# Another opening for a state-space and gated-unit kernel: single tiles, smaller first weight loads, tanh gates

## The chip, the cores and the metric

The kernel runs on one core of a Trainium2 chip. A core has five engines, each with its own instruction queue: TensorE (PE in the profile; PEld is its loading of weights), VectorE (DVE), ScalarE (ACT), GpSimd (POOL) and SyncE (SP, which here only issues transfers). They run side by side and wait for each other through semaphores. The on-chip memory SBUF feeds all of them; matrix products land in PSUM, which has eight banks. The metric is the device time of one execution in microseconds (us); lower is better.

## The reference

For 2048 tokens of width 448 the reference adds to the input the product of two branches, both computed from the layer-normed input:

```python
xn = (x - mean(x)) / sqrt(var(x) + 1e-5)

dt      = exp(log_dt)                          # branch s, 448 complex states
Lam_bar = exp(dt * Lam)
Bu      = xn @ (((Lam_bar - 1) / Lam)[:, None] * Bmat).T
h[t]    = Lam_bar * h[t - 1] + Bu[t]
s       = 2 * real(h @ Cmat.T) + xn * Dskip

g = silu((sigmoid(xn @ w_gate) * (xn @ w_up)) @ w_down)      # 1792 hidden columns

out = x + s * g
```

Inputs and output are bf16.

## The kernel before

**Tiles.** The 2048 tokens are four chunks of 512 (`TC`), a chunk is four tiles of 128 tokens, and half a chunk is `HC` = 256. The width 448 is three blocks of 128 rows and one of 64. For each chunk the kernel needs `xnT`, the normed input with its width on the partitions. Chunk 0's is made on PE (`ln_turn`, L268, identity products into the PSUM tile `tp_x`, then a copy to SBUF by VectorE in `ln_out`, L276); those of chunks 1 to 3 are made by transposing DMAs of SP (L265). The last 64 rows of `xnT` stand twice, in the upper and lower half of the partitions, so that products with 64 rows can run side by side in the two halves of PE. The hidden columns are 14 blocks of 128 (`ft`), each with a gate sum and an up sum in a PSUM bank of its own.

**Order.** The order on each engine is the order in which the code is written (`keep_order`, L52): every engine takes its instructions strictly one after the other, so an instruction that waits holds all that stand behind it on its engine.

**The opening** (L933 to L1016) prepares chunk 0 by hand. SP loads x in pairs of tiles (L133, L137), then the first 512 columns of the weights `wg`, `wu` and their last 64 rows `wt` (`load_w`), then the matrices `b_re` and `b_im`, then columns 512 to 1024, then x of chunk 1. ACT's queue loads three rows of parameters. While they come, PE multiplies the identity by itself (`warm`, L192). Means and variances of tiles 0 and 1 come from VectorE (`ln_stats`, L208 and L209), those of 2 and 3 from ACT's sums (L218 to L225); the root is a power on GpSimd (`ln_pow`, L238), one for two tiles. `ln_norm` (L256) writes the normed tile, `norm0` turns it.

In the same time cosines and sines of the state's angles are made for four blocks of states (`pt`), 256 steps each: a count of whole turns by ACT (`emit_whole`, L408) for blocks 0, 1 and 3, the fraction by VectorE (`emit_frac`, L427), for block 2 both on GpSimd (L414 to L419); the magnitude (L435), then sine and cosine on ACT (L440, L443). `emit_steps` (L323) does the same for two single angles, with the chain of small GpSimd operations that ends in `nf` (L330), VectorE's `anf` (L331) and two short sines. VectorE negates the sines (`emit_neg`, L452), GpSimd mirrors the 256 steps into the other half of the tables (`emit_mirror`, L455 to L458).

PE meanwhile sums the first four blocks of gates and ups in halves of 256 tokens (L705, L712). VectorE casts the up sums out of PSUM (`up_copy`, L1000), ACT takes the sigmoid of the gate sums (L717, after a load of its table, 1.28 us), VectorE multiplies (L722).

**The stream.** From L1078 on, `duo` runs two units side by side on the two halves of PE. A unit is one gate-and-up block (number 4 to 13 in chunk 0) or one block of the state's input product (`bu`, written as -1 to -4). A unit needs free banks: unit 4's are those that the first blocks' casts and gates free. The planner spreads VectorE's pieces (scans, rotations) among them; `at(chunk, unit, cost, fn)` hangs other work behind a unit. After unit 6 come the norms of chunk 1 with SP's four transposes, the load of C (`load_c`, L164) and that of `wd` (L1030), which the down products (`emit_downs`, L516 d_ps) at the head of chunk 1's line need whole.

**SP's list.** After the first loads SP issues: two transposes of `b_re` and `b_im` block 0 into `bT` (L291), the weights' columns 1024 to 1792, six more transposes, x of chunk 2, the four transposes of `xnT`, C, `wd`. The last 64 columns of `b_im` are first doubled by two copies (`emit_b_twice`, L282 and L283).

Of the kernel before, what the change touches and what calls it, by code (L numbers as in the profile page):

```python
# [63 lines left out]
def kernel(  # L64
# [35 lines left out]
    xnT = [w.tile([P, KT + 1, TC], BF16, name=f"xnT{c}") for c in range(3)]  # L100
# [32 lines left out]
    sync.dma_start(out=x_t[0][:, 0:2, :], in_=x_src[:, 0:2, :])  # L133
# [4 lines left out]
    load_w(sync, 0, 512)  # L138
# [11 lines left out]
    load_w(sync, 512, 1024)  # L150
    load_x(1)
    sync.dma_start(out=skip[:], in_=A_Dskip.partition_broadcast(P))
# [18 lines left out]
    pool.memset(xn[0][:, :, D:DP], 0.0)  # L171
# [71 lines left out]

    def ln_minus(c):
        t = slice(c * TPC, (c + 1) * TPC)
        dve.tensor_single_scalar(out=nmr[:, t, :], in_=mv[:, t, 0:1], scalar=-1.0, op=ALU.mult)
# [5 lines left out]
    def ln_norm(c, j):  # L252
        t = c * TPC + j
        xb = xn[c % 3]
        if c < 2:
            dve.tensor_scalar(out=xb[:, j, 0:D], in0=x_t[c][:, j, :], scalar1=mv[:, t, 0:1],  # L256
                              scalar2=rsd[:, t, :], op0=ALU.subtract, op1=ALU.mult)
        else:
            act.activation(xb[:, j, 0:D], x_t[c][:, j, :], ACT.Identity, bias=nmr[:, t, :],
                           scale=rsd[:, t, :])  # L260

    def ln_turn(c, j):
        xb, cols = xn[c % 3], slice(j * P, (j + 1) * P)
        if c > 0:
            sync.dma_start_transpose(out=xnT[c][:, 0:KT, cols], in_=xb[:, j, :])  # L265
            return
        for i, f0 in enumerate((0, P, 2 * P, 3 * P, D - P)):
            pe.transpose(tps[j][:, i, :], xb[:, j, f0:f0 + P], ident[:, :])  # L268
# [6 lines left out]
    def ln_out(j, tp, copy):  # L275
        copy(out=xnT[0][:, :, j * P:(j + 1) * P], in_=tp[:])  # L276
# [3 lines left out]
    def emit_b_twice():  # L280
        t = raw["b_im"]
        pool.tensor_copy(out=t[:, 0:3, D:DP], in_=t[:, 0:3, 384:D])  # L282
        pool.tensor_copy(out=t[0:64, 3, D:DP], in_=t[0:64, 3, 384:D])  # L283
# [20 lines left out]

    def emit_vecs():
        tp = ps.tile([P, KT, 4], BF16, name="tp_v", tag="bank", bufs=8)
        turn_twice(tp, rows, 3)
        vec = w.tile([P, KT, 3], FP32, name="vec")
        dve.tensor_copy(out=vec[:], in_=tp[:, :, 0:3])
        dt_b = w.tile([P, KT], BF16, name="dt_b")  # L310
        act.activation(dt_b[:], vec[:, :, 0], ACT.Exp)
        K.update(dt=dt_b, lim=vec[:, :, 1], lre=vec[:, :, 2])
# [10 lines left out]
    def emit_steps():  # L323
# [9 lines left out]
        sn, cs = col("sn", 2 * KT), col("cs", 2 * KT)  # L333
# [78 lines left out]
    def turns_2():  # L412
        K["turns"] = sp.tile([P, HC], FP32, name="turns", tag="tcs")
        pool.tensor_scalar(out=K["turns"][:], in0=iota_f[:], scalar1=K["turn"][:, 2:3], scalar2=None, op0=ALU.mult)  # L414

    def frac_2():
        f = sp.tile([P, HC], FP32, name="frac2", tag="tcs")
        pool.tensor_scalar(out=f[:], in0=K["turns"][:], scalar1=MAGIC, scalar2=-MAGIC, op0=ALU.add, op1=ALU.add)  # L418
        pool.tensor_tensor(out=f[:], in0=K["turns"][:], in1=f[:], op=ALU.subtract)  # L419
        K[2] = f  # L420

    def emit_frac(pt, both=True):
        if pt == 2:
            f = K[pt]
        else:
            f = sp.tile([P, HC], FP32, name="frac", tag="wv")
            dve.scalar_tensor_tensor(out=f[:], in0=iota_f[:], scalar=K["turn"][:, pt:pt + 1], in1=K[pt][:],  # L427
                                     op0=ALU.mult, op1=ALU.subtract)
        K[pt] = f
        if both:  # L430
            emit_abs(pt)
# [99 lines left out]
    def last_rows(c, h):  # L531

        return KT if c == 0 and h else 3

# [8 lines left out]
    def bu_unit(c, pt):  # L543
# [4 lines left out]
        def ops(h, cc, n):  # L548
            lo, hi = bu_cols(pt, cc)
            return [(sums[cc], (bT[HALF[h], kt, lo:hi], xnT[c][HALF[h], kt if kt < 3 else last_rows(c, h), :], 0, TC))  # L550
                    for kt in range(n)]
# [150 lines left out]
    def gu_halves(c, ft, gt, ut, first, n0=0, n1=TC):  # L702
        f0, f1 = ft * P, (ft + 1) * P
        for t, p0 in ((gt, 0), (ut, 64)):
            pe.matmul(t[:, n0:n1], lhsT=wt[p0:p0 + 64, f0:f1],  # L705
                      rhs=xnT[c][p0:p0 + 64, KT if c == 0 and p0 else 3, n0:n1], start=first, stop=not first)

    def gu_wholes(c, ft, gt, ut, first, n0=0, n1=TC):
        f0, f1 = ft * P, (ft + 1) * P
        for t, wm in ((gt, wg), (ut, wu)):  # L710
            for kt in range(3):
# [3 lines left out]
    def gu_out(c, ft, gt, ub):  # L715
        sig = fp.tile([P, TC], BF16, name="sig")
        act.activation(sig[:], gt[:], ACT.Sigmoid)  # L717
        emit_mul()

        def mul():  # L720
            h = fp.tile([P, TC], BF16, name="hF", bufs=18)
            dve.tensor_tensor(out=h[:], in0=sig[:], in1=ub[:], op=ALU.mult)  # L722
            hF[c, ft] = h
# [4 lines left out]
    def gu_unit(c, ft):  # L728
# [6 lines left out]
        def ops(h, i, tail):  # L735
            x = xnT[c]
            o = [(sums[i], ((wg, wu)[i][HALF[h], kt, f], x[HALF[h], kt, :], 0, TC)) for kt in range(3)]
            return o + [(sums[i], (wt[HALF[h], f], x[HALF[h], last_rows(c, h), :], 0, TC))] * tail
# [194 lines left out]
    act.activation(dummy[:], hpi[:], ACT.Exp)  # L933
    ln_sum(2)
    ln_sum(3)
    warm(26)
    ln_stats(0)
    ln_stats(1)
    ln_root(0, 2)
    emit_vecs()  # L940
    ln_mean(2, 2)
    warm(18)
    ln_square(2)
    ln_square(3)
    emit_angles()
    tps = []

    def norm0(j):
        tps.append(ps.tile([P, KT + 1, P], BF16, name="tp_x", tag="bank", bufs=8) if j < 2 else tps[j - 2])
        ln_norm(0, j)  # L950
        ln_turn(0, j)

    norm0(0)
    norm0(1)
    warm(11)
    for pt in (0, 1, 3):
        emit_whole(pt)
    turns_2()
    act.activation(K["r"][:], K["arg"][:], ACT.Exp)
    ln_out(0, tps[0], dve.tensor_copy)  # L960
    ln_root(2, 2, True)
    ln_out(1, tps[1], dve.tensor_copy)
    frac_2()
    emit_frac(0)
    emit_sin(0)
    emit_cos(0)
# [4 lines left out]
    emit_frac(1, False)  # L971
    norm0(2)
    norm0(3)
    emit_abs(1)
    emit_sin(1)
    emit_cos(1)
    ln_out(2, tps[2], dve.tensor_copy)
    ln_out(3, tps[3], dve.tensor_copy)
    gus.append((bank("g_ps"), bank("u_ps")))
    for ft in range(3):  # L980
        gu_halves(0, ft, *gus[ft], False, 0, HC)
    gu_wholes(0, 3, *gus[3], True, 0, HC)
# [5 lines left out]
    for pt in range(2, KT):  # L988
        emit_frac(pt)
        emit_sin(pt)  # L990
        emit_cos(pt)
    emit_steps()
    emit_b_twice()
    for pt in range(KT):
        emit_neg(pt)
        emit_mirror(pt)
    ubs = [fp.tile([P, TC], BF16, name="ub") for _ in range(4)]

    def up_copy(ft):
        dve.tensor_copy(out=ubs[ft][:], in_=gus[ft][1][:])  # L1000
# [3 lines left out]
    for ft in range(4):  # L1004
        gu_out(0, ft, gus[ft][0], ubs[ft])
# [5 lines left out]
    for pt in range(KT):  # L1011
        for cc in range(2):
            emit_b(cc, pt)
        if pt == 0:
            load_w(sync, 1024, F)
# [4 lines left out]
    at(0, 6, 0.0, lambda: ln_pow(TPC, TPC))  # L1020
    for j in range(TPC):
        at(0, 6, 0.41, lambda j=j: ln_norm(1, j))
    at(0, 6, 0.2, lambda: ln_twice(1, dve.tensor_copy))
# [5 lines left out]
    at(0, 6, 0.0, load_c)  # L1029
    at(0, 6, 0.0, lambda: sync.dma_start(out=wd[:], in_=B_w_down.rearrange("(ft p) d -> p ft d", p=P)))  # L1030
# [47 lines left out]
    emit_line(0, ((4, 5), (-1, 6), (7, 8), (-2, 9), (-3, 10), (11, 12), (-4, 13)))  # L1078
# [48 lines left out]
```

## Time and profile before

| what | us |
|---|---|
| median of 3 runs | 186.23 (186.06 to 186.54) |
| the profiled execution, its own time | 186.64 |
| its span, first to last instruction | 184.8 |
| first product of the gates (L712) | starts at 8.41 |
| last product of the hand-written opening | ends near 15.7 |
| start of the dense stream of products | 16.29 |
| first down product | 43.14 |
| busy: PE / VectorE / ScalarE / GpSimd | 178.9 / 162.9 / 114.2 / 26.0 |

All times on the profile's rows count from the first instruction. The share of the span that an engine is busy is a mean over stages with different limits: PE's 97% says that the stream is full, not what a change in the opening is worth. In a chain of waits each row gives start, length and who worked; in a timeline each row gives start, length, engine, line, operation and tiles, and in brackets how long the engine had been idle before and what ended that.

### The profile page before, as it was taken

What the parts mean: (1) busy time and instruction counts of PE and PEld (TensorE: products, weight loads), DVE (VectorE), ACT (ScalarE), POOL (GpSimd) and SP (SyncE); (2) the same over time, 40 slices, a digit from 0 to 9 for tenths busy, and PEclk for the clock granted to TensorE, in tenths of its full rate; (3) what the DMA queues carried; (4) which work ended last, traced back from release to release, by engine and by line L of the source; (5) the groups of instructions that cost most, each with busy time, mean ns of one, the idle gap of its engine ahead of it and who ended that gap; (6) DMA issues with size and microseconds to landing.
All of it is one profiled execution on the core that took longest, in us unless ns stands there. A gap on an engine that the chain in (4) does not pass through costs nothing.

```text
span 184.8 us, 4501 instructions
## 1 busy us (share of the span) xinstructions
PE 178.9 (97%) x1721; PEld 96.4 (52%) x1721; DVE 162.9 (88%) x331; ACT 114.2 (62%) x236; POOL 26.0 (14%) x63
## 2 busy tenths in 40 slices
PE   7899999999999999999999999999999999999992
PEld 6775555444544344655554445545654444656551
DVE  3689799989999949998999989799999989699494
ACT  3996757998687885997557757047038567142220
POOL 3799347303000000003000000000000000000000
PEclk9999999999999999999999999999999999999998
DMA  5999989996431113011141010020010001011102
GB/s 152 323 307 241 211 122 160 245 345 87 101 75 40 28 32 99 4 51 51 32 87 28 4 28 0 4 99 0 4 30 4 0 12 22 0 50 53 28 25 75
DMA packets 27643, 15.07 MB, mean 82 GB/s; under 512 B 16227, under 2 KB 27622, under 8 KB 27622
## 3 DMA queue, kind: packets, MB, share of 16 engines
q1 hardware_dynamic: 27616, 14.79, 34.5%
q8 instruction: 13, 0.21, 0.5%
q14 instruction: 8, 0.07, 0.1%
q10 hardware_dynamic: 6, 0.00, 0.0%
HBM read 8.49 MB, written 1.84 MB: 56 GB/s over the span
## 4 chain that ended last, share of the span: by engine, by line
PE 88%; DVE 3%; POOL 2%; DMA 2%; ACT 2%; issue 1%; SPq 0%
PE g_ps L516 24%; PE d_ps L516 23%; PE u_ps L516 21%; PE y_ps L516 11%; PE bu L516 10%; DMA x<-in_A_x_dram 2%; DVE spm L452 1%; ACT junk L225 1%; DVE sg L867 1%; ACT junk L218 1%; POOL frac L418 1%; DVE ub L1000 1%; POOL frac L419 0%; POOL rsd L238 0%; SPq L133 0%
## 5 line engine op out<-in xcount | busy, mean ns | idle before, releaser
L516 PE MATMUL u_ps<-xnT,wu 64*128 64x512 bf16 x312 | 65.7, 376 | 0.0
L516 PE MATMUL g_ps<-xnT,wg 64*128 64x512 bf16 x312 | 60.2, 376 | 0.2 <-DVE ub L1000 0.2
L750 ACT ACTIVATE sig<-g_ps 128x512 bf16<-128x512 f32 x52 | 29.1, 596 | 31.1 <-PE g_ps L516 31.0
L516 PE MATMUL bu<-xnT,bT 64*128 64x512 bf16 x196 | 45.6, 376 | 0.0
L516 PE MATMUL d_ps<-wd,hF 64*128 64x448 bf16 x448 | 43.7, 349 | 0.0
L516 PEld LDWEIGHTS <-hF 64*128 64x128 bf16 x448 | 24.1, 94 | 19.0 <-POOLq L518 0.7
L516 PEld LDWEIGHTS <-wu 64*128 64x128 bf16 x312 | 23.6, 94 | 18.8 <-POOLq L518 1.6
L516 PEld LDWEIGHTS <-wg 64*128 64x128 bf16 x312 | 21.7, 94 | 19.3 <-POOLq L518 1.6
L750 ACT CAST ub<-u_ps 128x512 bf16<-128x512 f32 x52 | 29.2, 606 | 0.0
L747 DVE TENSOR_TENSOR hF<-sig,ub 128x512 bf16<-128x512 bf16 x52 | 21.1, 415 | 2.5 <-ACT ub L750 2.4
L599 DVE TENSOR_TENSOR_SCAN wv<-r_col,st,ta 128x512 bf16<-128x512 f32 x18 | 22.7, 1275 | 0.1
L516 PEld LDWEIGHTS <-bT 64*128 64x128 bf16 x196 | 17.8, 94 | 9.6
L516 PE MATMUL y_ps<-ct,h 64*128 64x448 bf16 (+2 forms) x203 | 22.7, 343 | 0.0
L516 PE MATMUL g_ps<-xnT,wt 64*128 64x512 bf16 x52 | 19.6, 376 | 0.0
L516 PE MATMUL u_ps<-xnT,wt 64*128 64x512 bf16 x52 | 19.6, 376 | 0.0
L516 PEld LDWEIGHTS <-h 64*128 64x128 bf16 (+1 forms) x203 | 13.3, 95 | 8.2 <-issue 0.4
L580 ACT CAST bus<-bu 128x512 bf16<-128x512 f32 x24 | 14.3, 597 | 2.9 <-PE g_ps L516 2.9
L778 ACT ACTIVATE sigd<-d_ps 128x448 bf16<-128x448 f32 x12 | 6.6, 550 | 14.3 <-PE d_ps L516 14.3
L516 PEld LDWEIGHTS <-wt 64*128 64x128 bf16 x104 | 9.8, 94 | 5.6
L238 POOL TENSOR_TENSOR rsd<-ve,mhalf 128x4 f32<-128x4 f32 (+1 forms) x5 | 4.7, 949 | 52.0 <-DVE st L607 41.2
L837 DVE TENSOR_TENSOR o_t<-y_ps,xn 128x448 bf16<-128x448 f32 x12 | 6.9, 617 | 2.9 <-PE y_ps L516 2.9
L593 DVE TENSOR_TENSOR ta<-ta,tb 128x1024 bf16<-128x1024 bf16 x12 | 8.3, 689 | 0.3
(151 smaller groups left out, 220.8 us busy)
## 6 DMA issues: line engine op xcount, KB each, us to landing
wd<-in_B_w_down_dram SPq DMA_DIRECT2D x1, 1568.0 KB
x<-in_A_x_dram SPq DMA_DIRECT2D x3, 448.0 KB, 4.4
out_dram<-o_t SPq DMA_DIRECT2D x6, 224.0 KB, 2.1
wg<-in_B_w_gate_dram SPq DMA_DIRECT2D x2, 384.0 KB, 5.3
wu<-in_B_w_up_dram SPq DMA_DIRECT2D x2, 384.0 KB, 5.6
wg<-in_B_w_gate_dram SPq DMA_DIRECT2D x1, 576.0 KB, 4.5
wu<-in_B_w_up_dram SPq DMA_DIRECT2D x1, 576.0 KB, 6.6
bsw<-bus SPq DMA_DIRECT2D x8, 64.0 KB, 2.1
```

The costliest lines, as they stand in the source:

```text
L218: act.activation(junk[:], x_t[c][:, j, :], ACT.Copy, accum_out=sums[:, t, 0:1])
L225: act.activation(junk[:], x_t[c][:, j, :], ACT.Square, bias=mv[:, t, 0:1], scale=-1.0, accum_out=sums[:, t, 1:2])
L238: pool.tensor_tensor(out=rsd[:, t:t + n, :], in0=ve[:, t:t + n, :], in1=mhalf[:, 0:n, :], op=ALU.pow)
L418: pool.tensor_scalar(out=f[:], in0=K["turns"][:], scalar1=MAGIC, scalar2=-MAGIC, op0=ALU.add, op1=ALU.add)
L516: m = pe.matmul(self.t[:, n0:n1], lhsT=lhsT, rhs=rhs, start=self.done == 1, stop=self.done == self.n)
L580: empty = [lambda cc=cc: act.copy(out=bus[:, cc, :], in_=pst[cc][:]) for cc in range(2)]
L593: dve.tensor_tensor(out=T["ta"][:], in0=T["ta"][:], in1=T["tb"][:], op=add)
L599: dve.tensor_tensor_scan(out=T["wv"][:, cc, :], data0=rb, data1=T["ta"][:, cc, :], initial=(0.0 if c == 0 else st[pt][:, cc, :]), op0=mul, ...
L747: dve.tensor_tensor(out=h[:], in0=sig[:], in1=ub[:], op=ALU.mult)
L750: u.empty = [lambda: act.activation(sig[:], gt[:], ACT.Sigmoid), lambda: act.copy(out=ub[:], in_=ut[:])]
L778: act.activation(sigd[:], ds[j][:], ACT.Sigmoid)
L837: dve.tensor_tensor(out=o[:, i, :], in0=ys[c, j + 2 * i][:], in1=xb[:, i, :], op=ALU.add)
```

## The change

- Tiles 0 and 1 of x come in single loads, tile 1 through ACT's queue. Each gets a root of its own, and its `var + eps` is made by GpSimd (`ln_pow_of`). The 64 doubled columns are written by a second, short norm instruction, so that a tile needs four turns instead of five, and `xnT` of chunk 0 has four blocks like the others. All turns use one PSUM tile.
- The weights come in columns 0 to 384, 384 to 768 (both ahead of `b_re` and `b_im`), 768 to 1280 (after x of chunk 1) and 1280 to 1792.
- The copies that double `b_im` move from GpSimd to VectorE, ahead of the sign flip of block 0.
- Whole turns come from ACT for blocks 1 and 3 only; block 0's are made by three VectorE operations, block 2's by the same three on GpSimd, now behind the second power. The sine's table is loaded by a one-column Silu. The blocks run in the order 0, 1, 3, 2.
- The first four gates are `(tanh(g/2) + 1) * (u/2)` in place of `sigmoid(g) * u`. Tanh, sine and Silu share a table; that of sigmoid is loaded behind the four tanhs.
- 40 warm-up products in groups of 26, 6, 4, 4 instead of 55 in 26, 18, 11.
- In the stream the first pairs are (4, 5), (6, 7), (-1, 8) instead of (4, 5), (-1, 6), (7, 8), and the norms of chunk 1, C and `wd` hang behind unit 7 instead of 6.

```diff
-    sync.dma_start(out=x_t[0][:, 0:2, :], in_=x_src[:, 0:2, :])
+    sync.dma_start(out=x_t[0][:, 0, :], in_=x_src[:, 0, :])
+    act.dma_start(out=x_t[0][:, 1, :], in_=x_src[:, 1, :])
...
-    load_w(sync, 0, 512)
+    load_w(sync, 0, 384)
+    load_w(sync, 384, 768)
...
-    load_w(sync, 512, 1024)
     load_x(1)
+    load_w(sync, 768, 1280)
...
+    def ln_pow_of(t, n, var, scale):
+        pool.tensor_scalar(out=ve[:, t:t + n, :], in0=var, scalar1=scale, scalar2=EPS, op0=ALU.mult, op1=ALU.add)
+        ln_pow(t, n)
...
-            dve.tensor_scalar(out=xb[:, j, 0:D], in0=x_t[c][:, j, :], scalar1=mv[:, t, 0:1],
-                              scalar2=rsd[:, t, :], op0=ALU.subtract, op1=ALU.mult)
+            for o, f0, f1 in ((0, 0, D),) + ((D, 384, D),) * (c == 0):
+                dve.tensor_scalar(out=xb[:, j, o:o + f1 - f0], in0=x_t[c][:, j, f0:f1], scalar1=mv[:, t, 0:1],
+                                  scalar2=rsd[:, t, :], op0=ALU.subtract, op1=ALU.mult)
...
     def emit_b_twice():
         t = raw["b_im"]
-        pool.tensor_copy(out=t[:, 0:3, D:DP], in_=t[:, 0:3, 384:D])
-        pool.tensor_copy(out=t[0:64, 3, D:DP], in_=t[0:64, 3, 384:D])
+        dve.tensor_copy(out=t[:, 0:3, D:DP], in_=t[:, 0:3, 384:D])
+        dve.tensor_copy(out=t[0:64, 3, D:DP], in_=t[0:64, 3, 384:D])
...
+    def frac_by(eng, pt, tag):
+        t = sp.tile([P, HC], FP32, name="turns", tag=tag)
+        eng.tensor_scalar(out=t[:], in0=iota_f[:], scalar1=K["turn"][:, pt:pt + 1], scalar2=None, op0=ALU.mult)
+        f = sp.tile([P, HC], FP32, name="fracs", tag=tag)
+        eng.tensor_scalar(out=f[:], in0=t[:], scalar1=MAGIC, scalar2=-MAGIC, op0=ALU.add, op1=ALU.add)
+        eng.tensor_tensor(out=f[:], in0=t[:], in1=f[:], op=ALU.subtract)
...
-        sig = fp.tile([P, TC], BF16, name="sig")
-        act.activation(sig[:], gt[:], ACT.Sigmoid)
+        t = sp.tile([P, TC], FP32, name="tanh", tag=("ta", "tb")[ft % 2])
+        act.activation(t[:], gt[:], ACT.Tanh, scale=0.5)
...
-            dve.tensor_tensor(out=h[:], in0=sig[:], in1=ub[:], op=ALU.mult)
+            dve.scalar_tensor_tensor(out=h[:], in0=t[:], scalar=1.0, in1=ub[:], op0=ALU.add, op1=ALU.mult)
...
+    for t in range(2):
+        ln_stats(t)
+        ln_pow_of(t, 1, mv[:, t:t + 1, 1:2], 1.0)
...
+    act.activation(dummy[:], hpi[:], ACT.Silu)
+    ln_pow_of(2, 2, sums[:, 2:4, 1:2], 1.0 / D)
+    frac_by(dve, 0, "ta")
+    emit_abs(0)
+    emit_frac(1)
+    frac_by(pool, 2, "tcs")
...
+    emit_abs(1)
+    emit_b_twice()
+    emit_sin(0)
+    emit_cos(0)
+    emit_neg(0)
+    emit_frac(3)
+    emit_abs(3)
+    emit_abs(2)
+    emit_steps()
+    for pt in (1, 3, 2):
         emit_sin(pt)
         emit_cos(pt)
-    emit_steps()
-    emit_b_twice()
-    for pt in range(KT):
         emit_neg(pt)
+    emit_step_sines()
+    for pt in (0, 1, 3, 2):
         emit_mirror(pt)
...
-    emit_line(0, ((4, 5), (-1, 6), (7, 8), (-2, 9), (-3, 10), (11, 12), (-4, 13)))
+    emit_line(0, ((4, 5), (6, 7), (-1, 8), (-2, 9), (-3, 10), (11, 12), (-4, 13)))
```

## The prediction

> **What bounds the kernel now.** I read the windows first, then the chain of waits, then who waited for whom, then the timelines of SP, VectorE and GpSimd.
>
> ```profile
> 0.00:8.41 8.41, 6.39 (x71) 5.85 (x72) 4.03 (x21) 5.23 (x14) 4.28 (x15) 1.00 0.77 227
> 8.41:16.29 7.88, 7.63 (x76) 5.86 (x76) 7.29 (x19) 7.82 (x18) 7.25 (x19) 1.00 1.20 266
> 16.29:24.80 8.51, 8.51 (x80) 4.50 (x81) 7.37 (x22) 4.99 (x11) 4.37 (x12) 1.00 1.25 227
> 24.80:43.10 18.30, 18.30 (x168) 8.73 (x163) 17.27 (x37) 15.11 (x34) 8.28 (x19) 1.00 0.94 212
> ```
>
> ```profile
> 12.50 0.29 POOL nf L330
> ...
> 12.82 0.28 DVE anf L331
> 13.10 1.94 DVE spm L452 x4
> 15.04 1.21 DVE ub L1000 x2
> ...
> 16.29 0.80 PE g_ps L516 x5
> ```
>
> ```profile
> PEld L516 <- DMA wd<-in_B_w_down_dram: 0.5, 1, 0.5
> ```
>
> The windows (length, then busy time of PE, its loads, VectorE, ScalarE, GpSimd, the clock, the DMA share, GB/s) show PE without a hole from 16.29 us on. The kernel is therefore an opening of 16.29 us and a stream of matrix products that nothing shortens. The opening ends through GpSimd (the steps' fractions, L330), VectorE's four sign flips (L452) and two casts out of PSUM (L1000) that free banks. Behind 16.29 PE waits once: at 43.1 for wd, the weights of the down projection. Before it the products start 0.216 us apart; the last started at 42.75, so without wd the first down product would have come at 42.97 and came at 43.14. There is 0.17 us of lateness there already: an earlier opening is worth nothing unless wd lands earlier too, and a later wd is paid in full. What sends wd is SP:
>
> ```profile
> 11.04 2.07 SPq L291 DMA_TRANSPOSE bT<-b_re  x1
> 13.21 1.20 SPq L291 DMA_TRANSPOSE bT<-b_im  x1
> 14.46 0.58 SPq L122 DMA_DIRECT2D wg<-in_B_w_gate_dram  x1
> ...
> 16.80 1.27 SPq L291 DMA_TRANSPOSE bT<-b_re  x1
> ...
> 24.89 0.58 SPq L144 DMA_DIRECT2D x<-in_A_x_dram  x1
> 25.58 5.73 SPq L265 DMA_TRANSPOSE xnT<-xn  x4
> 31.41 0.53 SPq L164 DMA_DIRECT2D c_re<-in_A_C_re_dram  x1
> ...
> 33.58 0.50 SPq L1030 DMA_DIRECT2D wd<-in_B_w_down_dram  x1
> ```
>
> From 11.04 to 33.58 SP issues back to back: each row starts where the one before it ended (the transposes cost 1.2 to 2.1 us of SP each). So wd goes out 22.54 us after the first bT transpose, and that one was released by b_im: issued at 5.18, with 5.8 us to landing, 10.98.
>
> **The change, part by part.** Times are those of the profiled execution (span 184.8, its own time 186.64; the median of the runs is 186.23, so I carry the difference over to the median).
>
> *Tiles of x, roots, turns.* Tiles 0 and 1 come in two loads of 112 KB, one through ACT's queue. The load of both took 2.7 us from 0.72 (VectorE started at 3.46). Bounds: 3.46 again, or 0.72 + 1.7 (the 112 KB store at the end) = 2.4; I take 3.15, near its own row. Then statistics 0.63 + 0.18, GpSimd's add 0.24 (as L317) and its power, between half of 0.72 and 0.72 for one column, 0.55: root 0 at 4.95, root 1 one add and one power behind it on the same queue, 5.85. Norm 0.35 plus 64 columns 0.15, four transposes 0.45 to their end, a copy of 0.40 (0.49 for 640 columns): second copy done at 7.25 instead of 8.35, first product 7.3 instead of 8.41. The ACT queue's three rows are pushed back 0.50; PE reads them at 4.2, behind the 26 warm-ups, and VectorE needs them at 5.5: nothing.
>
> *Weights in 384 columns.* The first wu landed at 2.85 + 5.6 = 8.45 as KB number 1280 of the queue; now it is number 1072. From there to b_im (number 2072, 10.98) the queue moves 313 KB/us, so 208 KB less is 0.67: 7.8. Each DMA of the program takes one of eight counters in turn and is held until the load eight places ahead of it has landed (the second wg goes out at 6.87, when the first has come, 1.74 + 5.1). The first wu now stands eight behind a tile of x and goes out at 3.2 instead of 2.85; the bytes ahead of it keep the queue until 6.6, so that is hidden. The first wave ends near 9.8, the outs of tiles 2 and 3 near 11.1 (their root still waits for ACT's squares, 7.77), PE's opening at 14.7 instead of 15.66. This is the gain: about 1 us on PE. It is not what ends the opening.
>
> *What the second 384 columns do to b_im.* Before b_im stood 448 KB of x and 896 of weights; now 448 and 1344. 448 KB at 313 is 1.43 us: b_im lands at 12.4 to 12.5. A row says the same: in the kernel before, the second wg load ended at KB 2512, issued 6.87, 5.6 to landing, 12.47; b_im now ends at 2520. Two things hang on it. First SP: the bT transpose waits for that landing, 12.5 instead of 11.04. The list behind it to wd has the same issues (2 transposes, 4 weight loads, 6 transposes, x, 4 xnT, 4 C, wd), so wd is issued near 35.05. Bounds: +1.0 if the queue is faster than 313 by a quarter, +2.0 if 768-byte rows are slower by as much. Second, VectorE: the copies of b_im (L282, L283) move from GpSimd to VectorE, where they wait for that landing, and queued behind them are the sign flip of 0, the fraction and magnitude of 3 and the magnitude of 2, for which ACT's sines wait, and all PSUM casts. VectorE reaches them at 11.35 and leaves at 13.0.
>
> *The sines.* Fraction 3 (0.47) ends at 13.7, so ACT's sine of 3 starts at 13.75 (12.50 before). GpSimd's three steps for tile 2 (0.93, 1.30, 0.83) stand behind the power now, so nf ends near 13.6 instead of 12.79, and its copies of the mirror start then. Those hold VectorE:
>
> ```profile
> 13.01 2.02 DVE L452 TENSOR_SCALAR spm<-spm 128x256 bf16<-128x256 bf16 x4
> ...
> 13.27 0.39 POOL L455 COPY cosT<-cosT 128x255 bf16<-128x255 bf16 x1
> 13.61 0.39 POOL L457 COPY spm<-spm 128x255 bf16<-128x255 bf16 x1
> 13.95 0.39 POOL L458 COPY spm<-spm 128x255 bf16<-128x255 bf16 x1
> 14.29 0.39 POOL L455 COPY cosT<-cosT 128x255 bf16<-128x255 bf16 x1
> ```
>
> Four flips of 0.21 each took 2.02, and the row ends only after GpSimd's four copies did (14.68). If the magnitudes and anf are held in the same way, 1.4 us: the cosine of 3 at 15.2, four more activations at 0.35 to 0.40 and two short ones, the first tanh (0.60, as the sigmoid) from 16.85 to 17.45. Without the hold it ends at 16.1. The bank of unit 4 needs that tanh and one cast, so the dense stream starts at 16.15 (0.15 earlier) or 17.5 (1.2 later). I take 17.5, by the row. The Trainium skill, SBUF — State Buffer, section Who interferes with whom, calls the pair of ports that VectorE and GpSimd share an exclusive lock, held for a whole instruction. By that rule the holds are one copy each and the start could be 16.15; the row shows four copies in a row, and the row decides.
>
> The table load for sigmoid (1.28) moves behind the tanhs, to where ACT has 3 us until banks are needed again. The casts become multiplications by a half of the same shape, 0.68 as L1000. The four gate products become three-operand ones: 0.66 by L489 (0.68 for 448 columns) instead of 0.41, 1.0 in all on VectorE. Fewer warm-ups (40 for 55): if the array ran at half rate (26 warm-ups took 2.95 us, the last 11 took 0.78) for the first wave, 18 products would cost 0.11 more each, 2.0 us, and PE's opening would end at 16.7, still ahead of the tanh at 17.45. The Trainium skill, TensorE: Matmul & The Clock Gate, Part 1, says that full rate needs a busy window of some 3.4 us and that idle ones take it away; by it this 2.0 is possible, and hidden.
>
> *VectorE behind the opening.* Products and statistics of x1 end near 24.4, GpSimd's power 1.15, four norms and the copy 1.6: 27.3. SP asks for them at 25.58 + 1.45 = 27.0 (today: ready at 24.79, asked at 25.58). Adds 0.0 to 0.5; I take 0.2. The scan units come one pair later (-1 with 8), but VectorE waits there for PE, and PE for neither.
>
> *Sum.* wd later by 1.45 + 0.2 = 1.65: lands near 44.7. PE is there at 42.97 + 1.2 = 44.2 and waits. From 43.14 on everything moves by about 1.65: 186.23 + 1.65 = 187.9. The opening's own lateness is inside it, since both are paid at the same place.
>
> **Rivals.**
> 1. *VectorE is held a second time.* The flip of 2 comes after the sine of 2 (16.2), when GpSimd has six more copies queued (0.34 apart, to 18.0). Then the casts start at 18.05, the dense stream at 18.75, the norms of x1 end at 29.1, wd is later by 3.5: 189.7. For it: the row of 2.02. Against: a copy waits for the flip of 1, which opens a door.
> 2. *Gain and loss both hidden.* The queue catches up, b_im lands by 11.1, SP goes on as before, wd at 43.1: PE gains up to 0.5 us in the opening and gives it back at wd: 186.2. For it: the wait at wd exists today. Against: 448 KB more stand ahead of b_im and the DMA share in the opening is at 1.20.
> 3. *The other side: faster.* The queue is quicker with first loads in smaller pieces and the early start carries through: b_im by 10.5, no stop on VectorE, anf at 13.8 by nf, the dense stream at 15.7, SP's list 0.5 sooner and wd at 42.6: 185.6. It decides from the point at which b_im lands before 11.0. Against it is the same arithmetic.
>
> **How the numbers follow.** Forecast 0.59 (its own range 187.2 to 188.5, from wd +1.0 to +2.2), rival 1 0.15, rival 2 0.12, rival 3 0.14. A difference under 0.3% (0.56 us) can't be told from none here. Slower: forecast and rival 1, 0.74; within: rival 2, 0.12; faster: rival 3, 0.14. Range 186.2 to 189.2: it takes in rival 2 and the smaller half of rival 1.
>
> **What would show it.** Right: the first L714 product near 7.3; b_im's landing and the first bT transpose near 12.5; VectorE idle in front of the copy of b_im for a good 1 us; wd issued near 35 and PE idle ahead of the first d_ps product by 0.3 to 2 us more than now. Wrong: the first bT transpose at 11.2 or earlier, or wd landing before PE arrives; then the opening's start alone tells the time.

## The result and the profile after

The changed kernel took 189.37 us (median of 6 runs, 188.13 to 191.54) against 186.27 (6 runs, 185.54 to 186.54): 1.0138 times as long, 95% interval 1.0092 to 1.0184. Two of the six, at 191.5, are left out of the ratio (the other four have a median of 188.53); the profiled run is one of them, and its further loss (half clock behind a wait) is told below. In a second set of runs it took 188.81 against 186.41, ratio 1.0120 (1.0086 to 1.0154).

The same windows as before (length, busy PE, loads, VectorE, ScalarE, GpSimd, granted clock, DMA share, GB/s), and one more behind them, from the changed kernel:

```profile
0.00:8.41 8.41, 5.91 (x60) 5.03 (x61) 4.71 (x23) 5.40 (x15) 4.13 (x17) 1.00 0.70 203
8.41:16.29 7.88, 7.20 (x70) 5.15 (x69) 7.15 (x22) 5.88 (x15) 7.40 (x17) 1.00 1.11 308
16.29:24.80 8.51, 8.51 (x81) 4.46 (x79) 7.40 (x18) 6.83 (x13) 4.74 (x10) 1.00 1.31 188
24.80:43.10 18.30, 18.21 (x167) 8.73 (x163) 17.59 (x38) 15.13 (x34) 9.16 (x21) 1.00 0.87 205
43.10:60.00 16.90, 14.47 (x134) 7.02 (x136) 13.42 (x26) 10.56 (x21) 0.16 (x1) 0.90 0.65 99
```

PE is again without a hole from 16.29 to 43.0, and then idles 2.5 us; the clock of that last window is 0.90. Who was waited for (us in all, times, longest), the line that answers to the 0.5 of before, with the wait of the product itself:

```profile
PEld L520 <- DMA wd<-in_B_w_down_dram: 3.0, 1, 3.0
...
PE d_ps L520 <- DMA wd<-in_B_w_down_dram: 2.5, 1, 2.5
```

SP's timeline (start, length, operation), to be held against the rows of before:

```profile
11.91 0.58 SPq L154 DMA_DIRECT2D skip<-in_A_Dskip_dram  x1
12.62 1.36 SPq L299 DMA_TRANSPOSE bT<-b_re  x1
14.08 1.20 SPq L299 DMA_TRANSPOSE bT<-b_im  x1
15.33 0.58 SPq L122 DMA_DIRECT2D wg<-in_B_w_gate_dram  x1
...
17.47 1.51 SPq L123 DMA_DIRECT2D wt<-in_B_w_up_dram  x1
19.20 1.20 SPq L299 DMA_TRANSPOSE bT<-b_re  x1
...
27.92 0.58 SPq L146 DMA_DIRECT2D x<-in_A_x_dram  x1
...
33.83 0.53 SPq L166 DMA_DIRECT2D c_re<-in_A_C_re_dram  x1
...
35.99 0.49 SPq L1040 DMA_DIRECT2D wd<-in_B_w_down_dram  x1
```

The first bT transpose starts 1.58 us later than before (12.62 for 11.04), wd goes out 2.41 later (35.99 for 33.58) and lands at 45.5; PE arrived at 42.85, 0.12 earlier than before. The opening on VectorE, the rows around the copies of b_im and the sign flips:

```profile
12.28 0.21 DVE L290 COPY b_im<-b_im 128x192 bf16<-128x192 bf16 x1
12.76 0.17 DVE L291 COPY b_im<-b_im 64x64 bf16<-64x64 bf16 x1 [0.27 <-DMA b_im<-in_A_B_im_dram]
...
14.61 0.90 DVE L456 TENSOR_SCALAR spm<-spm 128x256 bf16<-128x256 bf16 x3
15.42 1.28 DVE L1010 TENSOR_SCALAR ub<-u_ps 128x512 bf16<-128x512 f32 x2
```

VectorE waits 0.27 for b_im, and three flips take 0.90, where four took 2.02 before. The first tanh starts at 15.46 and the dense stream at 16.15, 0.14 earlier than before. What ends the opening is now another thing; the chain of waits (start, length) runs through the second pair of copies into `xnT` and then through PE's own products:

```profile
11.38 0.77 DVE xnT L284 x2
...
16.15 1.02 PE g_ps L520 x7
```

One thing the prediction does not have at all. The end of VectorE's list, first of the kernel before, then of the changed one:

```profile
165.49 1.42 DVE L747 TENSOR_TENSOR hF<-sig,ub 128x512 bf16<-128x512 bf16 x4
166.83 0.68 DVE L616 TENSOR_TENSOR td<-wv,spm 128x1024 bf16<-128x1024 bf16 x1
...
169.41 1.28 DVE L660 TENSOR_TENSOR_SCAN wv<-r_col,st,ta 128x512 bf16<-128x512 f32 x1
...
173.39 0.42 DVE L671 TENSOR_TENSOR td<-wsw,spm 128x512 bf16<-128x512 bf16 x1 [2.24 <-DMA wsw<-wv]
```

```profile
169.56 1.43 DVE L750 TENSOR_TENSOR hF<-sig,ub 128x512 bf16<-128x512 bf16 x4
170.90 0.69 DVE L612 TENSOR_TENSOR tcs<-wv,cosT 128x1024 bf16<-128x1024 bf16 x1
171.50 0.69 DVE L616 TENSOR_TENSOR td<-wv,spm 128x1024 bf16<-128x1024 bf16 x1
...
174.08 1.28 DVE L660 TENSOR_TENSOR_SCAN wv<-r_col,st,ta 128x512 bf16<-128x512 f32 x1
...
178.43 0.43 DVE L671 TENSOR_TENSOR td<-wsw,spm 128x512 bf16<-128x512 bf16 x1 [2.61 <-DMA wsw<-wv]
```

In the changed kernel one product (tcs, L612, 0.60 us of VectorE) stands behind the gate products of the last chunk; before, it was done ahead of them. The last scan, the swap of its halves, and the outputs follow it. From the first down product to PE's last product it is 138.08 us in the kernel before, in a second profile of the changed kernel and in five of the experiments below (138.28 where PE comes to that product without a wait). So a span is the start of the first down product, plus 138.08, plus the end behind PE:

| kernel | first down product | PE's last product | end behind it | span |
|---|---|---|---|---|
| before | 43.14 | 181.22 | 3.62 | 184.84 |
| changed, first profile | 45.52 | 185.28 | 4.44 | 189.72 |
| changed, second set | 45.20 | 183.28 | 4.09 | 187.37 |

The second set is +2.06 at wd and +0.47 at the end, 2.53 in all. The first has 1.68 more between: ten steps behind the wait, from 46.10 to 49.68, are 0.24 to 0.37 us long, where down products otherwise start 0.19 apart. Not all of the longer end is the product. The issue of the second half of the swap by SP, first of the kernel before, then of the changed one:

```profile
171.23 0.60 SPq L541 DMA_DIRECT2D wsw<-wv  x1
...
175.90 0.97 SPq L541 DMA_DIRECT2D wsw<-wv  x1
```

So some 0.4 of the first profile's 4.44 is this issue; in the second set it took 0.64. Why it varies, no run shows.

### The profile page after: what moved, and what is told of

The parts are those of the page before. It is cut to its first block, busy times and chain, and to the rows that moved or that the text cites. A ratio compares the mean times of both kernels' runs of the same rounds, so it can differ in the third digit from the quotient of the medians.

```text
span 189.7 us, 4477 instructions
## 1 busy us (share of the span) xinstructions
PE 179.6 (95%) x1702; PEld 95.6 (50%) x1702; DVE 165.3 (87%) x337; ACT 114.3 (60%) x236; POOL 27.6 (15%) x64
## 4 chain that ended last, share of the span: by engine, by line
PE 68%; DVE 15%; DMA 8%; issue 3%; SPq 3%; POOL 1%; POOLq 0%; DVEq 0%
PE g_ps L520 18%; PE d_ps L520 18%; PE u_ps L520 15%; PE y_ps L520 8%; PE bu L520 6%; DMA wd<-in_B_w_down_dram 5%; SPq L273 2%; DVE xn L264 2%; DVE hF L750 1%; DMA x<-in_A_x_dram 1%; DMA wsw<-wv 1%; DVE sg L870 1%; DVE o_t L840 1%; POOL rsd L239 1%; SPq L166 1%
## 5 line engine op out<-in xcount | busy, mean ns | idle before, releaser
L520 PE MATMUL u_ps<-xnT,wu 64*128 64x512 bf16 x312 | 66.8, 376 | 0.0
L520 PE MATMUL g_ps<-xnT,wg 64*128 64x512 bf16 x312 | 59.0, 376 | 0.0
L520 PE MATMUL d_ps<-wd,hF 64*128 64x448 bf16 x448 | 45.3, 358 | 2.5 <-DMA wd<-in_B_w_down_dram 2.5
L520 PEld LDWEIGHTS <-hF 64*128 64x128 bf16 x448 | 24.7, 96 | 22.5 <-DMA wd<-in_B_w_down_dram 3.0
L520 PEld LDWEIGHTS <-wu 64*128 64x128 bf16 x312 | 24.1, 94 | 18.7 <-POOLq L522 1.7
L781 ACT ACTIVATE sigd<-d_ps 128x448 bf16<-128x448 f32 x12 | 6.7, 557 | 17.5 <-PE d_ps L520 17.5
L580 ACT CAST bus<-bu 128x512 bf16<-128x512 f32 x24 | 14.3, 596 | 2.9 <-PE bu L520 2.9
L239 POOL TENSOR_TENSOR rsd<-ve,mhalf 128x4 f32<-128x4 f32 (+2 forms) x6 | 5.9, 976 | 53.8 <-PE u_ps L520 49.7
```

The costliest lines, as they stand in the source:

```text
L239: pool.tensor_tensor(out=rsd[:, t:t + n, :], in0=ve[:, t:t + n, :], in1=mhalf[:, 0:n, :], op=ALU.pow)
L520: m = pe.matmul(self.t[:, n0:n1], lhsT=lhsT, rhs=rhs, start=self.done == 1, stop=self.done == self.n)
L580: empty = [lambda cc=cc: act.copy(out=bus[:, cc, :], in_=pst[cc][:]) for cc in range(2)]
L781: act.activation(sigd[:], ds[j][:], ACT.Sigmoid)
```

## The experiments

**a_weights_before**: all of the change, but the weight loads of before.

```diff
-    load_w(sync, 0, 384)
-    load_w(sync, 384, 768)
+    load_w(sync, 0, 512)
...
-    load_x(1)
-    load_w(sync, 768, 1280)
+    load_w(sync, 512, 1024)
+    load_x(1)
...
-            load_w(sync, 1280, F)
+            load_w(sync, 1024, F)
```

> The changed kernel with the weight loads of the kernel before: columns 0:512, then the two b, then 512:1024, x1, and 1024:1664 later; all else as changed. Theory (SP's list sets wd): four issues and 448 KB fewer stand ahead of the first bT transpose, so it starts at 11.0 to 11.6 instead of 12.62, wd is issued at 33.4 to 34.2 instead of 35.99, PE waits for it 0 to 0.7 us instead of 2.67, and the time is 186.0 to 186.9. The first up product waits for its weights until about 8.4. Rival (VectorE's new work, three-operand gate products and copies of b_im, is what delays, and the wait for wd only shows it): 187.7 or more with wd again at 35.5 or later.

187.51 us against 186.72, ratio 1.0044 (1.0016 to 1.0071). Most of the loss is gone, no wait for wd is left, but neither theory had the rest. SP's timeline:

```profile
10.79 1.30 SPq L298 DMA_TRANSPOSE bT<-b_re  x1
13.92 1.19 SPq L298 DMA_TRANSPOSE bT<-b_im  x1
...
34.94 0.50 SPq L1039 DMA_DIRECT2D wd<-in_B_w_down_dram  x1
```

(The last columns run to 1792, not to 1664 as the two expectations on the load order say.) The first transpose is back at 10.8, but the second, of b_im, starts 1.8 us after the first has been issued: VectorE made the copies of b_im that it needs only from 13.66 to 14.1, behind the turns of tiles 2 and 3. So the copies' move from GpSimd to VectorE costs SP time by itself where the loads do not. SP also waits until 27.31, 0.87 us, for the normed x of chunk 1, which VectorE finishes at 27.29. wd goes out at 34.94 and lands at 43.71; PE arrives at 43.91 in this profile, late by itself (below).

**a_b_first**: as many issues ahead of the first bT transpose as in the changed kernel, the two b nearer the front.

```diff
-    load_w(sync, 0, 384)
-    load_w(sync, 384, 768)
+    load_w(sync, 0, 512)
...
-    load_x(1)
+    load_w(sync, 512, 768)
+    load_x(1)
     load_w(sync, 768, 1280)
```

> The changed kernel with as many weight issues ahead of the first bT transpose as changed, but the two b ahead of columns 512:768 (loads 0:512, b_re, b_im, 512:768, x1, 768:1280). It parts two causes of the late first bT transpose. If it is b_im's landing behind more bytes, as the prediction had it, b_im lands near 11 and the transpose starts at 11.0 to 11.5, wd near 34.5, time 186.3 to 187.0. If it is the count of issues on SP (each half a microsecond, SP issuing without a stop from 3.4 to 12.5 in the changed kernel), b_im lands near 11 all the same, but the transpose starts at 12.4 to 12.7, wd near 36, time 187.8 to 188.8.

188.62 against 186.72, ratio 1.0132 (1.0078 to 1.0185). b_im landed at 10.58 and the first bT transpose started at 12.80 all the same: SP's twenty loads took until 12.68 to issue, with only two short pauses early on. Here it is the count of the issues, not b_im's landing, that holds the list. wd went out at 35.19 and landed at 43.62, and the first down product started at 43.67; the end behind PE was 4.61, with 1.14 for the second half of the swap. (The profiled run, 188.13, is the fastest of the six.)

**a_wd_before_c** and **b_wd_before_c**: in the changed kernel and in the kernel before, SP issues wd ahead of the four loads of C.

```diff
-    at(0, 7, 0.0, load_c)
     at(0, 7, 0.0, lambda: sync.dma_start(out=wd[:], in_=B_w_down.rearrange("(ft p) d -> p ft d", p=P)))
+    at(0, 7, 0.0, load_c)
```

> The changed kernel with wd issued by SP ahead of the four loads of C instead of behind them; nothing else. Theory (the whole loss is PE's wait for wd): issue near 33.8, landing near 41 to 42 because C's 900 KB are no longer in front, PE arrives at 42.85 and doesn't wait; time 185.8 to 186.2, no run above 187. Rival 1 (another late thing stands behind wd: VectorE, the swaps bsw, C's transposes): 187 or more, with a new wait of PE after 43. Rival 2 (wd still late at 43.3): 186.4 to 186.9.

> The kernel before with the same swap of wd and the loads of C. Theory: only its 0.17 us of wait goes, 186.0 to 186.2, so that the changed opening with the same swap stands at 0.1 us better or the same. Rival (wd's lateness is worth more than its wait, or C now comes late): 185.5 or less, or 186.8 or more.

The changed kernel: 188.57 against 186.72, ratio 1.0097 (1.0064 to 1.0130). wd landed at 41.10 and the first down product started at 42.31 without a wait, but C landed 5 us later (45.5 for 40.2), ACT waited 2.7 and 1.9 us for its transposes, and PE lost 0.8 us at 57 (two starts 0.36 and 0.87 us apart instead of 0.22) to casts of ACT behind them; the end was 4.25. Rival 1: the wait moved. The kernel before: 186.24 against 186.72, ratio 0.9976 (0.9951 to 1.0000), first down product at 42.53 without a wait.

**a_again**: the changed kernel itself, beside the next three.

> The changed kernel itself, beside the three that follow. Theory (three parts: wd late, one VectorE product more behind the last scan, the clock falling to half after PE's wait in some runs): PE waits for wd 1.0 to 2.7 us, 4.3 to 4.4 us from PE's last product to the end of the span (3.6 before), median 188.0 to 189.0, single runs up to 191.5. Rival (the first profile of it was an odd one): no wait over 0.7 us, and then the loss is elsewhere.

188.81 against 186.41. The wait for wd and the longer end are in the table above. New is the opening, PE's timeline (the wait in brackets):

```profile
4.84 0.21 PE L198 MATMUL tp_v<-ident,rows 3*128 3x3 bf16 x3 [0.55 <-DMA rows<-in_A_Lambda_re_dram]
...
8.10 0.80 PE L714 MATMUL g_ps<-xnT,wg 128*128 128x256 bf16 x3 [0.42 <-DVE xnT L284]
8.70 0.84 PE L714 MATMUL u_ps<-xnT,wu 128*128 128x256 bf16 x3
...
10.97 0.49 PE L714 MATMUL u_ps<-xnT,wu 128*128 128x256 bf16 x3
```

PE stops at 4.3 for the three rows, which ACT's queue sends 0.5 us later because of the tile of x. The array is then still at half rate when the gate products begin: a group of three takes 0.60 to 0.65 us from start to start until 10.62 and 0.33 after it. The dense stream starts at 16.97 instead of 16.15. The wait for wd hides it. In a_order_before the rows were waited for by 1.30, in a_weights_before by 1.37, and full rate came at 10.07 and 10.68.

**a_warm_wait**: 30 products of the identity ahead of the first down product.

```diff
         sums = [Sum(d, 2 * FT) for d in ds]
+        if c == 0:
+            for _ in range(30):
+                pe.matmul(ds[0][:, 0:P], lhsT=ident[:], rhs=ident[:], start=True, stop=True)
```

> The changed kernel with 30 products of the identity (some 1.7 us at full clock) put into PE's list ahead of the first down product, into the bank that it starts afresh; they run while PE waits for wd. Theory (idling there costs the clock in some runs): the ten products at 0.367 us apart of the first profile don't appear, no run above 189.8, median 0 to 0.5 below the changed kernel's. Rival (the spread up to 191.5 comes from wd's landing or from the opening): the same spread; if wd comes early in most runs, 0.5 to 1.5 slower.

189.66 (188.76 to 190.04), ratio 1.0163 (1.0134 to 1.0192): by the medians 0.85 slower than the changed kernel beside it (1.0120, 1.0086 to 1.0154), but the two intervals overlap. No run of either is at 191. In the profile wd landed at 44.62 and the first down product started at 44.81, so these products delayed it by 0.2 at most. Two of the six runs still had a mean granted clock of 0.991. The theory is not borne out. The rival's slowdown has the right size, but wd did not come early in the one profile, so whether the 0.85 is real, and where it comes from, is open.

**a_warm_open**: more products of the identity in the opening.

```diff
-    warm(26)
+    warm(30)
...
-    warm(6)
+    warm(9)
...
-    warm(4)
+    warm(10)
     ln_norm(0, 1)
     ln_turn(0, 1)
-    warm(4)
+    warm(14)
```

> The changed kernel with 63 instead of 40 products of the identity in the opening (30, 9, 10 and 14 for 26, 6, 4 and 4), which fill its four pauses before the first gate product at 7.7. Theory (a half-rate stretch in the opening is hidden by the wait for wd): median within 0.4 of the changed kernel's, and no stretch at half clock between 5 and 12 us in the profile. Rival (the opening's clock is what costs): 0.7 or more faster.

188.66 against 188.81 of the changed kernel beside it: no difference. Full clock came at 6.59, ahead of the first gate product, but the added products delay that to 8.45 (7.72 in the changed kernel's first profile). PE came to the first down product at 44.19, and wd at 44.32 hid that once more.

**a_order_before**: the stream's order of before.

```diff
-    emit_line(0, ((4, 5), (6, 7), (-1, 8), (-2, 9), (-3, 10), (11, 12), (-4, 13)))
+    emit_line(0, ((4, 5), (-1, 6), (7, 8), (-2, 9), (-3, 10), (11, 12), (-4, 13)))
```

with the norms of x1, C and wd at unit 6 again.

> The changed kernel with the stream's order of before: scan unit -1 beside unit 6, and the norms of x1, C and wd at unit 6. Theory: VectorE's product tcs of the last chunk is again done ahead of the outputs of chunk 2, so the end from PE's last product to the span's end goes from 4.35 to 3.7, 0.6 us; PE may wait up to 1.1 us for the first bT near 19.5 to 20.5, hidden by its wait for wd, which is as late as before; median 0.4 to 0.8 below the changed kernel's. Rival 1 (the end is longer for another reason): no shorter end. Rival 2 (the wait for bT comes through): 0.3 slower or more.

189.66 (188.20 to 192.29), ratio 1.0160 (1.0120 to 1.0200), which overlaps the changed kernel's 1.0120 (1.0086 to 1.0154): no difference is shown. It didn't settle its question. The tcs is ahead of the outputs again and the last scan ends 10.53 us ahead of PE's last product, as before; but in this profile the second half of the swap took SP 1.36 us to issue instead of 0.60, and the end was 4.22. The next but one asks the same in a cleaner way.

**b_weights_after**: the kernel before with only the changed weight loads.

```diff
-    load_w(sync, 0, 512)
+    load_w(sync, 0, 384)
+    load_w(sync, 384, 768)
...
-    load_w(sync, 512, 1024)
     load_x(1)
+    load_w(sync, 768, 1280)
...
-            load_w(sync, 1024, F)
+            load_w(sync, 1280, F)
```

> The kernel before with only the weight loads of the changed kernel: columns 0:384, 384:768, then the two b, x1, 768:1280, and 1280:1664 later. Theory (the longer list on SP ahead of the first bT transpose makes wd late, and nothing else of the change is needed for it): first bT transpose at 12.3 to 13 instead of 11.0, wd issued at 35.0 to 36.2, the first down product at 44.2 to 45.4 instead of 43.14, the end behind PE's last product unchanged at 3.6, time 1.1 to 2.3 above the kernel before. Rival (the changed kernel's loss comes from the moved copies of b_im and the later stream order): within 0.5 of the kernel before.

188.42 against 186.04, ratio 1.0104 (1.0072 to 1.0137). SP's timeline:

```profile
11.99 0.82 SPq L153 DMA_DIRECT2D skip<-in_A_Dskip_dram  x1
14.39 1.30 SPq L292 DMA_TRANSPOSE bT<-b_re  x1
...
33.81 0.53 SPq L165 DMA_DIRECT2D c_re<-in_A_C_re_dram  x1
...
35.98 0.49 SPq L1031 DMA_DIRECT2D wd<-in_B_w_down_dram  x1
```

wd goes out at 35.98, the first down product starts at 45.07 and the end is 3.65. The load order alone makes the loss at wd. That wd goes out at the same time as in the changed kernel is chance: the first bT transpose starts 1.8 us later than there, and later than the 12.3 to 13 expected, and the list behind it takes 21.59 us instead of 23.37. SP was done with its loads at 12.81 and then waited for b_im, issued at 7.53 with 6.8 us to landing, 14.3. GpSimd's copy waited for the same landing, and VectorE's flips ran before its copies began:

```profile
12.40 0.62 DVE L453 TENSOR_SCALAR spm<-spm 128x256 bf16<-128x256 bf16 x4
...
14.37 0.34 POOL L283 COPY b_im<-b_im 128x192 bf16<-128x192 bf16 x1 [2.08 <-DMA b_im<-in_A_B_im_dram]
```

So b_im's landing can hold the list too. Why it took 6.8 us here and 4.2 to 4.9 with the same loads in the changed kernel is open. (With the old stream order PE also waited 0.85 us for the first bT at 19, which is hidden by wd.)

**b_tcs_behind**: the kernel before with one VectorE product moved.

```diff
             for f in (p3, p4, p5):
                 later(0.69, f)
+            if c == NCH - 1 and pt == 2:
+                held.append(p3)
...
-            if i is None:
+            if i is None or pieces[i][1] in held:
                 break
```

> The kernel before with one VectorE product moved: tcs of the last chunk's third scan stays behind the outputs of chunk 2, where the changed kernel has it; the same instructions. Theory: the first down product stays at 43.1, the last scan ends 9.93 instead of 10.53 us ahead of PE's last product, the end behind that product goes from 3.62 to 4.04, time 0.3 to 0.5 above the kernel before. Rival (slack hides it): no difference, and the longer end of the changed kernel has another cause.

186.55 against 186.04, ratio 1.0029 (1.0011 to 1.0048). VectorE's end:

```profile
165.06 1.42 DVE L749 TENSOR_TENSOR hF<-sig,ub 128x512 bf16<-128x512 bf16 x4
166.40 0.68 DVE L612 TENSOR_TENSOR tcs<-wv,cosT 128x1024 bf16<-128x1024 bf16 x1
...
169.58 1.28 DVE L662 TENSOR_TENSOR_SCAN wv<-r_col,st,ta 128x512 bf16<-128x512 f32 x1
```

The last scan ends 9.93 us ahead of PE's last product, as in the changed kernel, and the end is 3.94 instead of 3.62. The one product costs 0.32 us in the profile, and 0.2 to 0.9 by the interval of the runs.

**a_all_undone**: the changed kernel with wd ahead of C (as in a_wd_before_c) and the products that read C later, the identity products of a_warm_open, and tcs ahead of the outputs (`early` holds that one product).

```diff
-    for i, by_act, by_dve in ((1, "down1", 2), (3, "down1", 2), (5, "down1", 3), (0, "down2", 5), (2, "down2", 6),
+    for i, by_act, by_dve in ((1, "down3", 3), (3, "down3", 3), (5, "down3", 4), (0, 2, 5), (2, 3, 6),
...
-        while pieces and room[0] > 0.0:
+        while pieces:
             i = ready()
-            if i is None:
+            if i is None or (room[0] <= 0.0 and pieces[i][1] not in early):
                 break
```

> The changed kernel, opening kept, with the three found costs taken out: wd ahead of C on SP, and the products that read C four units later so that its lateness holds nothing (the wait at 57 us); 63 instead of 40 products of the identity in the opening; tcs of the last chunk ahead of the outputs again. Theory: no wait of PE for wd, first down product at 42.3 to 43.0, end 3.6 to 3.7, so 185.8 to 186.5, level with the kernel before or up to 0.3% faster. Rival (a cost not found yet): 187 or more.

187.36 against 186.04, ratio 1.0073 (1.0044 to 1.0102). The rival: no wait for wd, the end at 3.72, but PE itself came to the first down product at 44.59. The rows were waited for by 0.51 again, full clock came at 8.92, the many identity products ran at half rate, and the first gate product started at 9.46. (The profiled run, 188.44, is the slowest of the six.)

**a_rows_first**: as a_all_undone, with ACT's queue for the rows alone.

```diff
-    act.dma_start(out=x_t[0][:, 1, :], in_=x_src[:, 1, :])
+    sync.dma_start(out=x_t[0][:, 1, :], in_=x_src[:, 1, :])
```

and 8, 5 and 10 identity products behind the first 30.

> As a_all_undone, with one more cost taken out: the second tile of x goes through SP, so that ACT's queue carries only the three rows, as before; 53 products of the identity (30, 8, 5, 10). Theory (the rows, pushed back by the tile of x, are waited for by PE at 4.3, and the pause keeps the clock at half until 9 to 11 us in many runs): PE's pause ahead of the rows' transposes is 0.2 or less, full clock by 8.2, first gate product by 8.1, first down product at 42.4 to 43.2 without a wait, end 3.7, time 185.7 to 186.5, level with the kernel before. Rival (the opening is longer by itself): first down product after 43.4 with full clock by 8.2, time 187 or more.

186.57 against 186.37, ratio 1.0005 (0.9986 to 1.0023), all twelve runs between 186.19 and 187.15. PE's timeline:

```profile
4.66 0.23 PE L198 MATMUL tp_v<-ident,rows 3*128 3x3 bf16 x3
...
8.02 0.49 PE L716 MATMUL g_ps<-xnT,wg 128*128 128x256 bf16 x3 [0.29 <-DVE xnT L284]
```

No wait for the rows, full rate from the first gate product, first down product at 42.75 without a wait, end 3.73. With these costs taken out, the changed opening is level with the kernel before, which still has its wd behind C. How much of the step from 1.0073 to 1.0005 is the rows and how much the ten identity products fewer, these two runs don't part. No version was found that beats both kernels by more than the interval: the best that was run is the kernel before with wd ahead of C, 0.9976 with an interval that ends at 1.0000, and against that one no gain of the changed opening is shown.

## The prediction, step by step

**Right: where the time is set, and the side.** PE has no hole from the dense start to wd, a later wd is paid in full and the opening is not. That is the constant 138.08, and b_weights_after makes the same wait with the old opening.

**Mis-sized: wd later by 1.65.** It was 2.38 in the first profile and 2.06 in the second. The term "the list behind it to wd has the same issues" took 22.54 us over from before; it was 23.37 and 23.25. The loads of the last columns now meet the eight counters: they go out at 16.04 and 17.47, just behind the landings of wg and wu of the third load at 16.02 and 17.45, and single issues take 1.3 to 2.4 us where their like take 0.5 or 1.3. The prediction had applied the rule of the counters to the first wu load and not here. The kernel before has slow single issues too (2.07, 1.54 and 1.80 us for transposes), so 22.54 was no fixed length: with the same issues it was 21.57 in a_warm_open and 22.86 in a_warm_wait. What makes single issues slow is open.

**Right number, half of the cause: the first bT transpose at 12.5.** It started at 12.62, but what held it last was not b_im's landing: that came at 12.1 (7.86 and 4.2 to landing), and SP was issuing until 12.50. In a_again the two are 12.7 and 12.80. a_b_first landed b_im at 10.58 and started at 12.80: there the four added issues, half a microsecond each, are enough by themselves. In b_weights_after the landing, at 14.3, held it 1.5 us longer than the issues. So the step has two limits close to each other; the prediction counted its bytes and not its issues.

**Wrong size: VectorE idle at the copies of b_im for over 1 us.** It was 0.27: VectorE came there at 12.28 instead of 11.35, since the transposes of tiles 2 and 3 were done at 11.4, behind two fractions that stand ahead of their norms on VectorE. What their move costs SP was not charged; a_weights_before shows it, 1.8 us, where the landing no longer covers it.

**Failed: flips held through four copies, first tanh at 16.85 to 17.45, dense start at 17.5.** The tanh started at 15.46 and the stream at 16.15, the figure given for one copy each; but at 16.15 it is PE's own opening that ends (below). The Trainium skill (SBUF — State Buffer, Who interferes with whom) has the lock held for a whole instruction; the changed kernel agrees, 0.90 for three flips beside copies of 0.4. The row of 2.02 was no accident, it stands in two more profiles of the old opening (b_wd_before_c, b_tcs_behind), and in b_weights_after, where GpSimd's copies start only at 14.37, the same four flips take 0.62: the copies did hold them. But it didn't carry over to another order; why one flip there lost to four copies is open. As wd hid the start, the error cost the forecast nothing.

**Too early: first gate product at 7.3, PE's opening done at 14.7, and "it is not what ends the opening".** They were 7.72 and 16.15, later than the 15.66 of before: the second wave waited for the turns of tiles 2 and 3, whose copies came at 11.4 to 12.1. So the gain of 1 us on PE did not come, and PE's opening is what ends the opening.

**Failed: pushed back rows cost nothing.** PE reads them in the middle of its warming up. The waits for them, up to 1.37 us, keep the array at half rate for the first gate products in four of the seven profiles of the changed opening with 40 identity products. The bound of 2.0 for half rate was in the prediction and rightly called hidden; once wd was out of the way, the rows and the identity products around them were the largest thing left (a_all_undone to a_rows_first, which changes both: the ratio falls from 1.0073 to 1.0005).

**Not needed: the 0.2 at x1's norms.** They were done at 26.3, SP asked at 28.6. Where SP is earlier the term is there and larger, 0.87 in a_weights_before.

**Missing: the end, and the clock behind the wait.** "From 43.14 on everything moves by about 1.65" overlooked that the planner's list for VectorE is filled by a running balance. Scan unit -1 one pair later in chunk 0 puts one product behind the last outputs (0.32 us in b_tcs_behind's profile, alone 1.0029); where the end was longer than 4.1, SP's slow issue of the swap came on top. And half clock followed the wait in the profiled run, 1.7 us, and by its time and its mean granted clock of 0.991 perhaps in one more of the six. The mean clock alone doesn't tell: a run with 0.987 took 188.19.

The forecast of 187.9 is 0.6 below the 188.53 above, and that it is so near is in part luck: the step that was wrong outright, the late dense start, was hidden behind wd; the late wd was right and too small by 0.4 to 0.7, and the end was missing. Rival 1's 189.7 lies among the measured times, but its mechanism didn't occur. Rival 3's condition, b_im before 11.0, was met in a_b_first and did not decide.

## What to carry to other kernels

Count a step's issues on the queue that sends it as well as its bytes: four loads more made a list late with its data long there (a_b_first), and in another run the data were later still (b_weights_after). Follow a changed order to the last instruction of every engine, since a planner that keeps a balance hands a shift in the first chunk on to the end. A wait is worth removing only with what stands behind it in view: a_wd_before_c took PE's wait away and found the next.

## What the runs showed of the hardware

The granted clock changes at steps 3.41 us apart, or whole multiples of that, and it goes with PE's busy time in the stretch ahead. The windows ahead of and in the half-clock stretch, of the changed kernel and of a_b_first (columns as above):

```profile
42.71:46.12 3.41, 0.90 (x11) 0.33 (x10) 3.34 (x9) 3.41 (x8) 0.47 (x2) 1.00 1.43 183
46.12:49.53 3.41, 3.41 (x22) 1.44 (x20) 3.34 (x6) 2.50 (x6) 0.00 (x0) 0.50 0.46 103
```

```profile
4.29:7.71 3.42, 1.70 (x28) 1.56 (x28) 2.51 (x10) 2.53 (x9) 2.08 (x7) 1.00 1.00 310
7.71:11.12 3.41, 3.32 (x16) 2.31 (x16) 3.02 (x10) 3.39 (x10) 2.90 (x4) 0.50 1.06 294
```

A stretch with PE busy for 0.90 or 1.70 of 3.41 us was followed by half clock; those with 2.24 (a_warm_wait, 4.86 to 8.28), 2.44 (b_weights_after, 42.28 to 45.69) and 2.45 (a_again, 41.38 to 44.79, with the wait for wd split over two stretches) were not. Busy time as the profile has it does not decide alone: at the end of a_order_before a stretch with 1.47 (180.74 to 184.15) kept full clock. The other way, full clock came behind stretches with 2.94 us and more (2.94 to 3.41, in all fourteen profiles; PE's ends are modelled) and not behind 2.04, 2.12, 2.87 and 2.90. The Trainium skill (TensorE: Matmul & The Clock Gate, Part 1) gives a free-running window of 3413 ns, which agrees, and has an idle window take full rate away; here 1.7 us of idling in one did (a_b_first). So a pause of 0.55 us at the wrong place can cost a whole window at half rate (a_again: 2.87 busy from 3.83 to 7.24, half rate until 10.66), and the same program may meet it in one run and not in the next.
